# Attention with a gated SwiGLU on one core: the key and query products woven between the value products, and the first row of maxima written before the attention starts

## The chip, the core and the metric

The kernel runs on one core of a Trainium2 chip. The metric is the device time in microseconds of one execution; lower is better.

## What is computed

From x (1 x 2048 x 512), after a layer norm of each row:

```python
def _A_ref(x, wqkv, wo):                       # H = 32 heads, Dh = 16
    q, k, v = qkv[0], qkv[1], qkv[2]
    scores = jnp.einsum("bhqd,bhkd->bhqk", q, k) * Dh ** -0.5
    p = _softmax(scores, axis=-1)
    return einsum("bhqk,bhkd->bhqd", p, v).transpose(...).reshape(B, S, D) @ wo

def _B_ref(x, w1, w3, w2):                     # F = 1792
    return (_silu(x @ w1) * (x @ w3)) @ w2

xn = _layernorm(x)
return x + _A_ref(xn, wqkv, wo) * _silu(_B_ref(xn, w1, w3, w2))
```

All products are kept near f32 by splitting each operand into a high and a low part and multiplying three times (lo by hi, hi by lo, hi by hi).

## The kernel before, in words

**Two stages.** A prologue loads and normalises x in 16 tiles of 128 tokens, forms the value rows of all heads, and the key and query rows of the first 8 heads (two products of 512 tokens each per block). Then one long attention stage runs to the end, in which scores, row maxima, values and the whole gated feed-forward network share TensorE.

**The prologue (lines 449 to 693).** The 16 tiles make 4 blocks of 512 tokens. For each tile, `spread` takes mean and variance (VectorE, then a power on GpSimd), `norm` scales it (VectorE for the first tiles, ScalarE after), `transposed` turns it on TensorE and splits the result: the high part by a ScalarE copy, the low part by a VectorE subtraction. `token_values(b, i)` is one value product: 12 matmuls of 128x512; ScalarE copies the result out and its own DMA queue stores it. `token_rows(b, c)` is one key (c = 1) or query (c = 0) product of a block: 12 matmuls; ScalarE copies it out and GpSimd splits it (for the last block ScalarE and VectorE do). `keep_rows` stores these rows to DRAM, and `load_k`, `load_q` read them back, six DMAs each, into the layout that the scores need: everything that the first pair of heads multiplies goes through this round trip. `keep_tokens` stores a whole block of transposed tokens (two DMAs of 1 MB). These DMAs are on SyncE's queue.

**The order.** Block 0's four value products come first, inside the loop over the first four tiles. Then `for b in range(TB)` runs block by block: keys of the block, queries of the block, then (for blocks 1 to 3) its four value products. Between them `beside(b, n)` issues *maxima*: the shift of the softmax needs the row maximum of the scores, so `max_unit` (line 411) forms a 128x512 piece of the scores on half of TensorE and VectorE reduces it. 64 such units belong to the first half of the first pair of heads; the table `groups` spreads them in groups of 4, and two groups of 8 near the end. When all 64 are there, `max_rows` (line 424) reduces them, negates them on ScalarE, transposes them on TensorE, splits them and writes them by four DMAs as two more rows under the queries. Only then may the scores of the softmax itself be formed.

**The attention stage (from line 695).** The order in which TensorE gets its work is written out by hand in the table `ORDER_OF_ISSUE`, one letter per item: `f`/`F` a feed-forward matmul on the lower or upper half of the array, `m`/`M` a maximum unit, `s`/`S` a score product (line 706) with its exponential on ScalarE, `v` one chunk of value products (line 722, eight records), `R`/`r` the transposition of a row of maxima, `o` an output product. Small and capital letters stand for the two halves, which run side by side. TensorE takes its instructions in that order and waits where an operand is not there. A planner (`Model`) only decides buffers and small side tasks. The results of a letter stand in one of seven PSUM banks until VectorE or ScalarE has taken them out. Before, `rows` starts with the first row of maxima still to be transposed: the table's first `R` does it.

```python
for b in range(TB):              # lines 643 to 693, cut
    token_rows(b, 1)             # keys
    token_rows(b, 0)             # queries
    for i in range(TB):
        run(token_values(b, i))  # blocks 1 to 3
        beside(b, 2 + i)
```

Of the kernel before, what the change touches and what calls it, by code (L numbers as in the profile page):

```python
# [51 lines left out]
    "MfMfMfMfMffMfMfMffMffMfMfMffRfMfmFFfFmFFfFffFffFmFFFmFfffMfMfMmfFFFfFffFffFFFssfFmFFFffMfSffMsFFmfFS"  # L52
    "fFmSfFfSfMsFfmFsFfFFmsFFmMmvvsMfSfMfSfFFmSfFmFsFmFfSfMfFsFFfsMfSFfmFfFfMfSfMfSfSffMFsFfmFsFmFsFFfmFs"
    "FmFfSfFFmmMvvSmmMSmvvSmfSfMfSfMfSfmFsFFfmSFfsFmFsfFMsfFmFSfFmFfSmFfMmvvsMsSsSvvRmSfSfMFfsFfMfSFfsFmF"
    "SffMFsfFmSfFFmsFFfsMsFfsMvvsSSsmMvvFmsFmFsFFsFmfFfSfMSffMfSfFMfsFMffSffFSmFFffMSffmFFsFmFsfFsFMFfsFm"
    "sFFfMsFfMFffSfMfMmvvSssSmFmFvvSmMmMsvvMsFmFsfFsFfMSffFmSFfSfmSFffMfSFfmfFFfMfSfMfSfSffMsFfFmFsFFmsFF"
    "fmFsFmFsFFffMfMMfmSvvSmsMMmvvsMmFFsFfFsfMsFfFmSfFSfmFSfFfsMFfFfmFfMfMmMvvvRfSfMfSfMfSfMFfsFFmfSsFFfm"
    "FsFfFmSfFmFsFfFfMmMvvmSfFmSsFFffMFsfFmSFfsFmFFsfMFsfFmSFfMffMffSmMvvvFmsFmFFsFsFmsFmFFffSFmSFfMffSfM"
    "fSffMFfMMffMsvvmSfSfMfSfFFmfSFfMsFfsFMsfFFmsFFFmsFfMFffMfSmMvvsMmSFfFfFsfMFsFfmSfSfFmFsFfMsfFmFSfFmF"
    "fSfMfMmvvsMSfMfFsFffMsFfFmSFfFsmFFsFfmSFffSmFfSfFSsvvvvRfSMffSfMSffMfFsFmFfSFfFsmFsFFfmSFfFmsFFfMfmM"  # L60
    "vvmSSfmFfFFsfMFsFfmSFffSmFsFfFmSfFfMsFFffMSfMfmMvvSmMmsSvvMfSfMfSfMfSfMffSfSfMffMsFFfsFmFFsFmFsFfFmS"
    "fmFFssFFfMfSfFmSfFfMsfFsFMfSFfmSfFfMsFfMFfMffMmMvvvMmMssMvvmSmFsFsFmFFmFsFfFsfFFmSfFmFssFFfMfSfFmsFF"
    "fMsfFfMSfSFfmFfFfMfSfMfSSffMffMfSsMvvsSSmmMvvmFFsMmmSvvRsFFmFsFmFsFmFsFmFsFmFsFfSffFMsfFfMSFffSmFfSf"
    "MSffFmSfFMffFMfSfffMSfSffMMsvvsSsSsSvvvFmsFmFFsFsmFsFmFFsFmFsFFmFsfFFfmSFfFsmFfSfMfSfFmFMfffSfSfMMmv"
    "vMmMmSsvvmSFmFssFfFfMsFFfmSfFfSmFSfFfmSFffMfSfFfMFffMfSMffSfsFfMsFfFmFsFmFsFfFmFsFmFfFfMfMmMvvvmSSss"
    "MvvRsFFmFsFmsFFsmFfFSffMfSfFmSFffMsFFffMfMMfSmvvsMSfMfSffMffSfMsFfFmFsFmFfSsFFfmFFsfFmSFffFfMfSfMSff"
    "fMsFFmfFFsmFFsmFFfSfmFFsFmfFMmvvmSmMmSvvSmmMsSvMfSfMffSfMfSffSfMFsfFmSFfmFsFFsFmSffFMsfFFmFFffMfSfMf"
    "SfFsfFMsfFmFsFfFmFFsmFsFfFFmfMMfMmvvvvvmSfMfSfSfFFmfSfFMsfFFsMsFFfmfSFfMsfFmFSfFFffMSfffSfMSfmFfFFsm"
    "FsFFfmFsFFmFsfFFmSfSfrvvsMSfSmfFfFfMFsfFmSFfFsmFsFfMsfFmFSfFmFfMffMMmvvvsSSmSmvvMsfSMffSfFFmfSfFMsfF"
    "sFMsFFfmsFFMfsFFfmFMffMmMvvvSmMffFfSFffMFsmFfSFfFsmFFsFfSmfFmSfFFffMSffMfSffMfSfFsFmFsFfMsFFfmFsFmFs"  # L70
    "FfFFmMfMfMmvvvvsMfSmFfFFsfMsFFfmSFffSmFFsfMfSFfmSFffMFfFfMfSfffMSffMsFFsfFFmsFFmFsfFMfSfFsFmFfsFsSvv"
    "vvRMsFsmFFfFsfFmSFfsFmFsFfMSfFfmFFfMfSfffMSSffMfMffMmMvvvSmfMSffSfSfMfMffSfMfSfFFsmsFfFMsfFmFsFFmFsF"
    "sFFfmsFfFMsfFmFSfFFsmFsfFMSffMfSffFSffMfMmMvvvmSmMmSvvmFFsFmFsmFFssFmFFffSFmSFfmFsfFfMSfFSfmSffFMsFF"
# [73 lines left out]
def raw(ap):  # L147
    return ap.bitcast(F32)
# [1367 lines left out]
```

## Time and profile before

| what | value |
|---|---|
| time, median of 3 runs (lowest, highest) | 1715.81 us (1714.9, 1715.91) |
| time of the profiled execution | 1717.6 us |
| its span, first to last instruction | 1715.8 us |
| mean granted clock of TensorE | 0.997 |
| busy share: TensorE, VectorE, ScalarE, GpSimd | 99%, 80%, 72%, 51% |
| DMA | 181.07 MB, mean 106 GB/s |

The profiled execution's own time is 1.8 us above its span and 1.8 us above the median. A busy share of TensorE counts every matmul from its start to its modelled end, with matmuls overlapping, so 99% doesn't say that it works at its full rate: the spacing of matmul starts says that.

### The profile page before, as it was taken

The page shows a single profiled execution, that of the slowest core. Times are in us where ns is not written, and L with a number is a line of the kernel's source. Part 1 is how long each engine was busy: PE and PEld are TensorE (multiplying, and loading weights), DVE is VectorE, ACT ScalarE, POOL GpSimd, SP SyncE. Part 2 cuts the span into 40 slices and gives each one's busy share as a digit, 9 for nine tenths or more (in the row PEclk, how much of TensorE's full clock was granted, in tenths as well). Part 3 has the DMA queues.
Part 4 walks back from the last instruction along what each step waited for, and adds up shares of the span by engine and source line. Part 5 has one row for each costly group of instructions (what it writes and reads, how often), then busy time and mean ns, then how long its engine had stood idle before and what let it go on. Part 6 is the DMA issues. An engine that isn't in the chain of part 4 may idle for free.

```text
span 1715.8 us, 35891 instructions
## 1 busy us (share of the span) xinstructions
PE 1700.4 (99%) x13476; PEld 1125.9 (66%) x13476; DVE 1376.2 (80%) x2295; ACT 1228.0 (72%) x2446; POOL 868.4 (51%) x911
## 2 busy tenths in 40 slices
PE   8999999999999999999999999999999999999998
PEld 6766666666766666666666666666667666665456
DVE  5788888898887888887897888778788787889626
ACT  4338777777767777778777777777777777868870
POOL 7155463466456653565546762565366616653011
PEclk9999999999999999999999999999999999999999
DMA  7563433443344443422244452321433312421264
GB/s 261 200 206 93 125 96 86 106 114 59 87 153 104 118 96 100 106 64 59 83 119 123 129 124 82 97 70 51 105 91 77 81 38 61 116 78 30 81 208 145
DMA packets 170893, 181.07 MB, mean 106 GB/s; under 512 B 43872, under 2 KB 115552, under 8 KB 167744
## 3 DMA queue, kind: packets, MB, share of 16 engines
q1 hardware_dynamic: 167552, 172.76, 37.0%
q10 hardware_dynamic: 3168, 6.03, 1.0%
q8 instruction: 106, 1.74, 0.5%
q14 instruction: 67, 0.55, 0.1%
HBM read 131.56 MB, written 46.11 MB: 104 GB/s over the span
## 4 chain that ended last, share of the span: by engine, by line
PE 92%; issue 2%; DVE 2%; DMA 2%; SPq 1%; POOL 1%; ACT 0%; ACTq 0%; DVEq 0%; POOLq 0%
PE f L1023 32%; PE pv L722 26%; PE m L419 16%; PE e L706 15%; PE m L546 2%; DVE mp L421 1%; DMA wr<-in_A_wqkv_dram 1%; SPq L758 0%; DMA ovh<-o 0%; PE m L434 0%; DMA inh<-in_A_x_dram 0%; PE e L201 0%; PE m L519 0%; PE o L201 0%; PE e L205 0%
## 5 line engine op out<-in xcount | busy, mean ns | idle before, releaser
L421 DVE TENSOR_REDUCE mp<-m 128x1 f32<-128x512 f32 x2048 | 1277.6, 683 | 216.0 <-PE m L419 139.9
L709 ACT ACTIVATE pt<-e 128x512 f32<-128x512 f32 x2048 | 1058.4, 612 | 281.7 <-PE e L706 162.4
L419 PE MATMUL m<-ks,qs 62*128 62x512 f32 x2048 | 741.9, 413 | 4.7 <-DMA qs<-qk 3.2
L706 PE MATMUL e<-qs,ks 64*128 64x512 f32 x2048 | 737.6, 407 | 0.0
L722 PE MATMUL pv<-pt,vt 128*17 128x512 f32 x4096 | 479.5, 594 | 0.0
L419 PEld LDWEIGHTS m<-ks,qs 62*128 62x128 f32 x2048 | 349.3, 184 | 123.6 <-issue 39.3
L706 PEld LDWEIGHTS e<-qs,ks 64*128 64x128 f32 x2048 | 349.4, 185 | 101.9 <-issue 34.9
L722 PEld LDWEIGHTS pv<-pt,vt 128*17 128x17 f32 x4096 | 100.2, 97 | 251.0 <-issue 245.0
L1023 PE MATMUL f<-xtl,wh 64*128 64x512 f32 x504 | 183.9, 392 | 0.0
L1023 PE MATMUL f<-xth,wl 64*128 64x512 f32 x504 | 178.9, 394 | 0.0
L1023 PE MATMUL f<-xth,wh 64*128 64x512 f32 x504 | 175.7, 392 | 0.0
L1023 PE MATMUL f<-wh,hs 64*128 64x512 f32 x528 | 165.8, 392 | 0.0
L866 POOL TENSOR_TENSOR h<-g,h 128x512 f32<-128x512 f32 x56 | 72.1, 1287 | 182.5 <-ACT h L862 182.4
L1023 PE MATMUL f<-xth,xel 64*128 64x512 f32 x440 | 160.5, 394 | 0.0
L1023 PE MATMUL f<-xth,xeh 64*128 64x512 f32 x440 | 160.5, 393 | 0.0
L1023 PE MATMUL f<-xtl,xeh 64*128 64x512 f32 x440 | 160.4, 391 | 0.0
L340 POOL TENSOR_TENSOR wl<-wr,wh 128x512 fp32r<-128x512 f32 x105 | 135.2, 1288 | 8.8
L1023 PE MATMUL f<-xeh,hs 64*128 64x512 f32 x368 | 121.3, 395 | 0.4 <-POOL hs L868 0.4
L340 POOL TENSOR_TENSOR xel<-wr,xeh 128x512 fp32r<-128x512 f32 x87 | 112.1, 1289 | 7.3
L339 POOL TENSOR_SCALAR xeh<-wr 128x512 fp32r<-128x512 f32 x87 | 53.8, 619 | 100.6 <-PE m L419 42.6
L1023 PE MATMUL f<-wl,hs 64*128 64x512 f32 x264 | 97.3, 392 | 0.0
L1023 PEld LDWEIGHTS f<-wh,hs 64*128 64x128 f32 x528 | 92.3, 185 | 4.8 <-POOL hs L868 1.0
(241 smaller groups left out, 2134.6 us busy)
## 6 DMA issues: line engine op xcount, KB each, us to landing
wr<-in_B_w_dram SPq DMA_DIRECT2D x168, 256.0 KB
qs<-qk SPq DMA_DIRECT2D x186, 64.0 KB
ks<-qk SPq DMA_DIRECT2D x90, 128.0 KB
ovh<-xt SPq DMA_DIRECT2D x36, 256.0 KB
ovl<-xt SPq DMA_DIRECT2D x36, 256.0 KB
wr<-in_A_wqkv_dram SPq DMA_DIRECT2D x30, 256.0 KB
qk<-ch SPq DMA_DIRECT2D x24, 256.0 KB
qk<-c SPq DMA_DIRECT2D x24, 256.0 KB
```

Source lines behind the costliest of these rows:

```text
L339: nc.gpsimd.tensor_scalar(hi, t, 1.0, 1.0, op0=ALU.mult, op1=ALU.mult)
L340: nc.gpsimd.tensor_sub(lo, t, raw(hi))
L419: nc.tensor.matmul(ps, qs[p % 2][64 * h:64 * h + KM, q0:q0 + P], ks[p % 2][64 * h:64 * h + KM, c * 512:(c + 1) * 512], start=True, stop=True)
L421: nc.vector.reduce_max(mp[p, half][:, h, qt, c:c + 1], ps, axis=AX.X)
L546: nc.tensor.matmul(ps, lhs, wv[k][h == 1], start=n == 0, stop=n == len(three) - 1)
L706: nc.tensor.matmul(ps, ks[p % 2][64 * h:64 * h + KR, k * P:(k + 1) * P], qs[p % 2][64 * h:64 * h + KR, q0:q0 + 512], start=True, stop=True)
L709: done = nc.scalar.activation(pt, ps, AF.Exp, scale=DH ** -0.5)
L722: nc.tensor.matmul(pv[32 * j:32 * j + VW, :], vt[2 * p // GH][:, key, 2 * p % GH + j % 2, :], pt, start=key < 2 if last else k == 0, stop= ...
L866: nc.gpsimd.tensor_mul(h2, g, h2)
L1023: nc.tensor.matmul(ps, left[r], right[r], start=starts and lane == 0, stop=ends and lane == 1)
```

## The change

The prologue's loop is replaced by a `plan`: a list of twenty products (key, query, value), each with the tiles to be turned after it, the number of maxima to be issued after it, and the small tasks then due. The key and query products of all blocks now stand between value products: k0 q0 v v k1 q1 v k2 q2 v v k3 q3 v v v and four more v. The value products still go in the order of the blocks. The 64 maxima come in twelve groups of 3 to 6. The first row of maxima is finished in the plan: its maximum and negation after the 17th product, its transposition and its DMAs after the 18th; the attention stage starts with `ready = {0: 0.5}` and no row to do. The last block's tokens and rows are split on GpSimd; `norm` of tiles 1 to 3 goes to ScalarE; one weight's split goes from GpSimd to VectorE; `keep_tokens` issues on ScalarE's queue instead of SyncE's; `vrow` has four buffers instead of two; block 1's tokens have buffers of their own. The table `ORDER_OF_ISSUE` is wholly new: the same number of `f`, `m`, `s` and `o`, 512 `v` and `r` as before, and 31 `R` and `r` for 32. Its letters form 200 runs of `v` and `r` where there were 206. Of the table the first line of either version is shown; the removed loop is cut, since the kernel before shows it.

```diff
@@ -49,98 +49,98 @@
 
 
 ORDER_OF_ISSUE = (
-    "MfMfMfMfMffMfMfMffMffMfMfMffRfMfmFFfFmFFfFffFffFmFFFmFfffMfMfMmfFFFfFffFffFFFssfFmFFFffMfSffMsFFmfFS"
...
+    "MffSfMfSfMSffMSffSMffSffMfsMffMfMfMsFFfsFFffFsFFmsFFsFfmSFffMFffMfSfSffMFsfFmFsFmFsFmFFfsFFmfSmFFfMf"
...
 )
 
 
@@ -497,7 +497,7 @@
             rs = pro.tile([P, 1], F32, tag="rs", name="rs", bufs=6)
             nc.gpsimd.tensor_tensor(rs, ve, minus, op=ALU.pow)
             nb = None
-            if t >= TB:
+            if t > 0:
                 nb = pro.tile([P, 1], F32, tag="nb", name="nb", bufs=6)
                 nc.gpsimd.tensor_scalar(nb, mv[:, 0:1], rs, -1.0, op0=ALU.mult, op1=ALU.mult)
             of[t] = mv, rs, nb
@@ -513,14 +513,20 @@
         def transposed(t, xn):
             b, tt = divmod(t, 4)
             if tt == 0:
-                xts[b] = xt_pair(keep) if b % 2 else rows2 if b else even_pair()
+                xts[b] = rows2 if b == 2 else (even_pair, lambda: xt_pair(pro), None, lambda: xt_pair(keep))[b]()
             ps = bank("m")
             for k in range(KC):
                 nc.tensor.transpose(ps[:, k * P:(k + 1) * P], xn[:, k * P:(k + 1) * P], ident)
             hi, lo = (v[:, :, tt * P:(tt + 1) * P] for v in xts[b])
             src = ps.rearrange("p (k t) -> p k t", k=KC)
-            nc.scalar.copy(hi, src)
-            nc.vector.tensor_sub(lo, src, raw(hi))
+            if b < TB - 1:
+                nc.scalar.copy(hi, src)
+                nc.vector.tensor_sub(lo, src, raw(hi))
+            else:
+                xc = pro.tile([P, KC, P], F32, tag="xc", name="xc", bufs=2)
+                nc.scalar.copy(xc, src)
+                nc.gpsimd.tensor_scalar(hi, xc, 1.0, 1.0, op0=ALU.mult, op1=ALU.mult)
+                nc.gpsimd.tensor_sub(lo, xc, raw(hi))
 
         def split_w(i, sub=None):
             w = wraw.pop(i)
@@ -548,8 +554,8 @@
                     yield
             t = b * 4 + i
             v = ps.rearrange("p (h d) -> p h d", h=H)
-            nc.scalar.copy(vrow[t % 2][:, :, 0:DH], v)
-            nc.scalar.dma_start(v_d[t], vrow[t % 2].rearrange("p h d -> p (h d)"))
+            nc.scalar.copy(vrow[t % 4][:, :, 0:DH], v)
+            nc.scalar.dma_start(v_d[t], vrow[t % 4].rearrange("p h d -> p (h d)"))
             nc.scalar.copy(vt[0][:, t, :, 0:DH], v[:, 0:GH, :])
 
         nc.gpsimd.memset(raw(ks[0]), 1.0)
@@ -561,10 +567,10 @@
         spread(1)
         transposed(0, xn.pop(0))
         busy(6)
+        split_w(2)
+        split_w(3, nc.gpsimd)
         norm(1)
-        split_w(2, nc.gpsimd)
-        split_w(3, nc.gpsimd)
-        vrow = [pros.tile([P, H, VW], F32, name=f"vrow{i}") for i in range(2)]
+        vrow = [pros.tile([P, H, VW], F32, name=f"vrow{i}") for i in range(4)]
         for v in vrow:
             nc.gpsimd.memset(v[:, :, DH:VW], 1.0)
         nc.gpsimd.memset(room_v(0)[:, :, :, DH:VW], 1.0)
@@ -576,13 +582,12 @@
             if t < 3:
                 transposed(t + 1, xn.pop(t + 1))
             norm(t + 2)
-            if t < 2:
-                split_w(KC + t, nc.gpsimd)
+            if 0 < t < 3:
+                split_w(KC + t - 1, nc.gpsimd)
             for n in range(2):
                 load_x(8 + 2 * t + n)
-            if t > 1:
-                nc.gpsimd.memset(*next(blank))
             run(products)
+        nc.vector.memset(*next(blank))
         nc.vector.memset(pv, 0.0)
         for n in range(2):
             nc.vector.tensor_add(picks[:, 2 * n:2 * n + 2], each[:, 0:2], each[:, 2:4])
@@ -590,18 +595,7 @@
         early = [(c, qt, h) for c in range(4) for qt in range(8) for h in range(2)]
         early.sort(key=lambda e: (max(e[0], e[1] // 4), e[0] < e[1] // 4, e))
         early = iter([(0, 0, 4 * qt + c, h) for c, qt, h in early])
-        groups = {(1, 1): 4, (1, 2): 4, (1, 4): 4, (1, 5): 4, (3, 3): 8, (3, 4): 8}
-        groups.update({(2, n): 4 for n in range(6)})
...
         first_rows = max_rows(0, 0)
-
-        def beside(b, n):
-
-            for _ in range(groups.get((b, n), 0)):
-                max_unit(*next(early))
-            if (b, n) == (TB - 1, 4):
-                next(first_rows)
-                next(first_rows)
 
         def token_rows(b, c):
 
@@ -611,14 +605,10 @@
                 run(split3(ps, [w[:, k, :] for w in wqk[c]], (hi[:, k, :], lo[:, k, :]), k == 0, k == KC - 1))
             sh = pros.tile([P, 512], F32R, tag="sh", name="sh", bufs=3)
             sl = pros.tile([P, 512], F32R, tag="sl", name="sl", bufs=3)
-            if b == TB - 1:
-                nc.scalar.copy(sh, ps)
-                nc.vector.tensor_sub(sl, ps, raw(sh))
-            else:
-                sc = pros.tile([P, 512], F32, tag="sc", name="sc", bufs=2)
-                nc.scalar.copy(sc, ps)
-                nc.gpsimd.tensor_scalar(sh, sc, 1.0, 1.0, op0=ALU.mult, op1=ALU.mult)
-                nc.gpsimd.tensor_sub(sl, sc, raw(sh))
+            sc = pros.tile([P, 512], F32, tag="sc", name="sc", bufs=2)
+            nc.scalar.copy(sc, ps)
+            nc.gpsimd.tensor_scalar(sh, sc, 1.0, 1.0, op0=ALU.mult, op1=ALU.mult)
+            nc.gpsimd.tensor_sub(sl, sc, raw(sh))
             made_rows[b, c] = sh, sl
 
         made_rows = {}
@@ -629,68 +619,67 @@
 
         def keep_tokens(b):
             for s in range(2):
-                nc.sync.dma_start(raw(xt_d[b][s]), raw(xts[b][s]).rearrange("p k t -> p (k t)"))
+                nc.scalar.dma_start(raw(xt_d[b][s]), raw(xts[b][s]).rearrange("p k t -> p (k t)"))
 
         def more_tokens(n):
 
-            if n < NT:
-                transposed(n, xn.pop(n))
-                if n + 2 < NT:
-                    norm(n + 2)
-                if n + 4 < NT:
-                    spread(n + 4)
-
-        for b in range(TB):
-            cols = slice(b * 512, (b + 1) * 512)
-            last = b == TB - 1
-            token_rows(b, 1)
...
+            transposed(n, xn.pop(n))
+            if n + 2 < NT:
+                norm(n + 2)
+            if n + 4 < NT:
+                spread(n + 4)
+
+        def cols(b):
+            return slice(b * 512, (b + 1) * 512)
+
+        def keys_here(b):
+            return lambda: keep_rows(b, 1), lambda: load_k(0, cols(b))
+
+        def queries_here(b):
+            return lambda: keep_rows(b, 0), lambda: load_q(0, 0, cols(b)) if b < TB // 2 else None
+
+        def blank_next():
+            nc.gpsimd.memset(*next(blank))
+
+        def weights_first():
+            wts.pump(KC)
+            wts.fill()
+
+        plan = [
+            ("k", 0, (4, 5), 0, keys_here(0)[:1]),
+            ("q", 0, (6,), 0, ()),
+            ("v", 0, (7,), 0, queries_here(0)[:1] + keys_here(0)[1:] + queries_here(0)[1:]),
+            ("v", 1, (8,), 0, (lambda: keep_tokens(0),)),
+            ("k", 1, (9, 10), 0, ()),
+            ("q", 1, (11,), 4, keys_here(1)),
+            ("v", 2, (12, 13), 5, queries_here(1) + (lambda: keep_tokens(1),)),
+            ("k", 2, (14,), 5, ()),
+            ("q", 2, (15,), 5, keys_here(2)),
+            ("v", 3, (), 6, queries_here(2)),
+            ("v", 0, (), 6, (blank_next,)),
+            ("k", 3, (), 6, (lambda: load_q(1, 0), lambda: keep_tokens(2))),
+            ("q", 3, (), 6, keys_here(3)),
+            ("v", 1, (), 6, queries_here(3) + (lambda: load_q(0, 1),)),
+            ("v", 2, (), 6, (blank_next, blank_next, wts.start)),
+            ("v", 3, (), 6, (weights_first,)),
+            ("v", 0, (), 3, (lambda: next(first_rows), lambda: next(first_rows))),
+            ("v", 1, (), 0, (lambda: next(first_rows), lambda: next(first_rows, None))),
+            ("v", 2, (), 0, ()),
+            ("v", 3, (), 0, ()),
+        ]
+        done = 0
+        for what, n, tiles_, maxima_, then in plan:
+            if what == "v":
+                run(token_values(1 + done // TB, n))
+                done += 1
             else:
-                keep_rows(b, 1)
-            if b == 0:
-                keep_tokens(b)
...
+                token_rows(n, int(what == "k"))
+            for _ in range(maxima_):
+                max_unit(*next(early))
+            for t in tiles_:
+                more_tokens(t)
+            for e in then:
+                e()
 
     ring = ctx.enter_context(tc.tile_pool(name="ring", bufs=1))
     work = ctx.enter_context(tc.tile_pool(name="work", bufs=1))
@@ -1264,12 +1253,12 @@
 
 
 
-    ready = {}
+    ready = {0: 0.5}
     opened, closed = [], []
     count = {"S": 0, "M": 64, "V": 0, "chunks": 0, "phase": 1}
     keys = {0: 0.0}
     rooms = []
-    rows, outs = [[3.0, first_rows, 2, 0]], []
+    rows, outs = [], []
     stored = {}
     pv_free = 0.0
     multiplied = {}
```

## Rows read from the trace of the kernel before

**Rows 1.** Who waited for whom, PE, 130 to 1650 us: us, times, longest

```profile
PE f L1023 <- POOL hs L868: 0.4, 1, 0.4
```

**Rows 2.** The chain that ended last, in order: start us, us, what

```profile
124.74 1.84 PE pv L722 x16
...
199.44 2.70 PE pv L722 x24
```

**Rows 3.** Timeline of PE, 15 to 48 us: start us, us, engine line op, [idle before]

```profile
15.94 0.50 PE L546 MATMUL m<-wvl,xeh 128*128 128x512 f32 x1 [0.84 <-ACT xeh L522]
...
31.17 0.50 PE L201 MATMUL e<-xth,wkl 128*128 128x512 f32 x1 [1.48 <-ACT xth L522]
32.39 0.50 PE L203 MATMUL e<-xtl,wkh 128*128 128x512 f32 x1 [0.72 <-DVE xtl L523]
...
40.15 0.47 PE L419 MATMUL m<-ks,qs 62*128 62x512 f32 x1 [1.76 <-DMA qs<-qk]
42.05 1.19 PE L419 MATMUL m<-ks,qs 62*128 62x512 f32 x3 [1.43 <-DMA qs<-qk]
...
44.51 0.63 PE L546 MATMUL m<-wvl,xth 128*128 128x512 f32 x1
...
47.07 0.63 PE L546 MATMUL m<-wvl,xth 128*128 128x512 f32 x1
```

**Rows 4.** Stretches: us, PE, PEld, DVE, ACT, POOL busy, PEclk, DMA share, GB/s

```profile
29.00:31.00 2.00, 0.69 (x7) 0.46 (x5) 1.67 (x5) 2.00 (x5) 1.14 (x4) 1.00 1.04 416
...
41.00:48.00 7.00, 5.95 (x17) 4.48 (x18) 3.86 (x8) 1.30 (x2) 1.24 (x4) 0.51 0.58 194
```

**Rows 5.** Timeline of PE, 79 to 104 us: the first matmul of six products

```profile
79.83 0.50 PE L546 MATMUL m<-wvh,ovl 128*128 128x512 f32 x1
...
83.44 0.50 PE L201 MATMUL e<-xth,wkl 128*128 128x512 f32 x1
...
90.67 0.50 PE L546 MATMUL m<-wvh,xtl 128*128 128x512 f32 x1
...
93.53 0.39 PE L546 MATMUL m<-wvh,xtl 128*128 128x512 f32 x1
...
98.22 0.50 PE L546 MATMUL m<-wvh,xtl 128*128 128x512 f32 x1
...
103.07 0.50 PE L546 MATMUL m<-wvh,xtl 128*128 128x512 f32 x1
```

**Rows 6.** Timeline of PE, 106 to 119 us: the entry into the attention stage

```profile
106.00 0.50 PE L1023 MATMUL f<-xth,xel 64*128 64x512 f32 x1
...
111.75 0.28 PE L434 MATMUL m<-ident,nm 128*16 128x128 f32 x1
...
117.19 0.39 PE L1023 MATMUL f<-xtl,xeh 64*128 64x512 f32 x1
...
118.11 0.39 PE L1023 MATMUL f<-xth,xeh 64*128 64x512 f32 x1
...
118.39 0.39 PE L706 MATMUL e<-qs,ks 64*128 64x512 f32 x1
```

**Rows 7.** Timeline of DVE, 97 to 127 us

```profile
97.49 9.11 DVE L421 TENSOR_REDUCE mp<-m 128x1 f32<-128x512 f32 x15
...
113.94 0.27 DVE L438 TENSOR_TENSOR ml<-m,mh 16x128 fp32r<-16x128 f32 x1
```

**Rows 8.** Timeline of SyncE's issues (SPq), 33 to 87 us

```profile
33.14 4.05 SPq L398 DMA_DIRECT2D ks<-qk  x6
...
78.97 3.47 SPq L325 DMA_DIRECT2D wr<-in_A_wqkv_dram  x2
86.61 0.37 SPq L325 DMA_DIRECT2D wr<-in_B_w_dram  x1
```

**Rows 9.** The page, costliest groups: a split on POOL, count, busy us, mean ns

```profile
L340 POOL TENSOR_TENSOR wl<-wr,wh 128x512 fp32r<-128x512 f32 x105 | 135.2, 1288 | 8.8
...
L339 POOL TENSOR_SCALAR xeh<-wr 128x512 fp32r<-128x512 f32 x87 | 53.8, 619 | 100.6 <-PE m L419 42.6
```

More of the change, by code (lines that the diff above doesn't have):

```diff
@@ L57 @@
[L57 to L61, printed above, removed]
@@ new lines @@
+    "vRsMfMFsfFfSfFmFSfFmSffFFmFfFmFmmFmFvvvMfSfMffSfMfSffSfMsFFfmSfFFmsFsFFmfFSfMFsFfmFFfMffSMffSfSffMsF"
+    "fFmFsFFmsFfFmFsFFmsFFfMfMfMfmMvvvsMsMfFFfFsfMsFFfmSfFsFmFfSfMsfFFmSFfmFfMffMmMvvvSmfSfMSffFFmfSFfMsF"
+    "fsFMsFFfmsFfFMsFfmFFffMMmSvvmSsFmFsFFffMsFfFmSfFSfmFSffMfSFfmSFfsfFMFfmmMvvRSmsFFfmFsFFfmSFfFsmFFsfM"
+    "sFfFmSffMFfMfMfSmvvmSmSMmvvMsMffSSffMfSffMsFfFMfsFFmfSfSFfmFFsFmFsfFMsFFffMfSffMSffMsFFmFsFsFfMfFsFm"
+    "sFFfMsFFfmFMffMmMvvSmsSFmFmvvvSmsFmFfFfSfMsFfFmSfFfSmSFffMSfFfmFFffMfSfMfSffSfMsFFfmFsFFmsFFfmFsFFms"
@@ new lines @@
+    "FfFfMfMfSmMvvvSmSmsMvvvRSmfSFffMfSfFMsFfSfMsFFfmSffFMsFMfFfsFFmsFFffMsfFFmsFFfMsFfmFFsmFFfSfMFfsMfFf"
+    "FMfMfmMvvSmfSmFFfFsfMsFFfmSfFfSmFfSFfmSFfFmsFFffMSfSfsMvvmSsMMmvvmSMmSsvMfSffMSfMffSfMfSSffMfMfsFFfF"
+    "smFsFFmFsfFFmSfmFFssFfFMsFfFmSfFfMsFFfsMfSFfmSFfMffFfMfMmMvvvSssSsMvvSmsMMmvvfMfSMffSMffSfsFFmFFsfMs"
+    "fFmFFsFmFsFfSfMfSFfmFsFmFsFfSfFmSfFfMsFfFmFfSfMfSfMfFmrvmSSssMvvsMmMmSvvmSmFFsfFFsfMsFfMfSfMfFsFmFfS"
+    "sFfFmFfSfMsFfmFFsFmfFSfmFFsmFFfSffMFffSfMfSfMMmvvMsmMSsvmFsFFmFsmFFsmFFsFmFsFfSFffMsfFmFSfsFFmFsFfMf"
@@ L144 @@
+    "MfMMmvvvMsMfFsFfFsfMFsFfmSfFfSmFsFFfmSfFFmsFSfFfmFfSfMFsfFmFsFfMsFfFFsmSvsMmMsSvSmMffSMsvsMmSSmvSmmS"
+    "SfMfvMsMsMsvsMMffSsMvRMsFmSsvmSsSMmvmSmSMsvmSsSMmvmSMsmFSvSmmSSmvFmFsFmFssFFmFmFsSmvMsSmmSvmSsFsMosS"
+    "mFsMvSmSssMvsSSsMoSsmSvvSsSsmMvSmMmFsFsFFsMFsFMsFFMSsMvMsMSMSsSvsSsMMsvMSMSsvMsMSSsvsMSSSSSSvvvvRooS"
+    "sSssFosSsSSsvSsSsosSSsSsovSsSsSsovvSssSsSoSsSssSooovvvvsSsSSsSvovsSSssSovSsSsSsoSsSssSooooooovvvvv"
 )
@@ L592 @@
         early = iter([(0, 0, 4 * qt + c, h) for c, qt, h in early])
-        groups = {(1, 1): 4, (1, 2): 4, (1, 4): 4, (1, 5): 4, (3, 3): 8, (3, 4): 8}
-        groups.update({(2, n): 4 for n in range(6)})
-        groups.update({(3, n): 4 for n in range(2)})
         first_rows = max_rows(0, 0)
-        def beside(b, n):
-            for _ in range(groups.get((b, n), 0)):
-                max_unit(*next(early))
-            if (b, n) == (TB - 1, 4):
-                next(first_rows)
-                next(first_rows)
         def token_rows(b, c):
```

206 lines of the change are left out of this document (77 added, 129 removed).

## The prediction, written before the changed kernel was run

> **What bounds the kernel now.** I read the page first: TensorE counts as busy for 99% of the span, every other engine for 80% or less. Then who waited for whom on TensorE alone: in the 1520 us from 130 us on it idles visibly for less than a microsecond [rows 1]. So the attention stage runs at TensorE's pace, and what a letter of the table costs there is the spacing of matmul starts: 0.23 us on each half of the array, 0.115 us per half matmul (four steps from 117.19 to 118.11 us) [rows 6], and 0.86 us per chunk of values plus 0.12 us for each run of them (1.84 us for two, 2.70 us for three) [rows 2]. The change alters none of the counts of letters that matter. What it can win lies in the first 120 us, and the timeline of TensorE shows there what is lost.
>
> It is lost in four places. (a) Between 29 and 42 us TensorE stands four times: 1.48 + 0.72 us for block 1's turned tiles, then 1.76 + 1.43 us for the first queries on their way through DRAM [rows 3]. That is 5.4 us. The order causes it: keys and queries of two blocks are formed with nothing else to do, and the first maxima follow at once. (b) After that idling the granted clock falls: 0.51 over 41 to 48 us, the lower of the two levels (1.2 GHz, not 2.4) [rows 4]. Value matmuls start there every 0.43 us (six from 44.51 to 47.07) [rows 3] instead of 0.24 us (twelve from 90.67 to 93.53) [rows 5]. (c) The two groups of eight maxima: a value product with a group of four takes 3.61 us (79.83 to 83.44), one alone 2.86 us, one with a group of eight 4.85 us (98.22 to 103.07) [rows 5]. So four maxima cost 0.75 us, eight 1.99 us. (d) The entry into the attention stage: from 106.00 to 118.39 us, the first score, TensorE goes through 77 letters [rows 6], 76 half matmuls and one transposition of a row.
>
> **The change, part by part.**
>
> *Waits (a).* In the plan two value products and three tiles stand between q0 and k1, and k1 and q1 before the first maximum. Block 1's last tile then has a value product and a tile ahead of k1, 3 us, where it was late by 1.5 us. From q0 to the first maximum the kernel before has k1, q1 and a few tiles, and waits 5.4 us in all until 42.05 us; now two value products stand there besides, 2 x 2.86 us [rows 5]. They cover the waits with 0.3 us to spare. Gain 5.4 us; ends 2.2 us, if only the turned tiles come in time, and 5.4 us. A remainder of the wait is charged below.
>
> *Clock (b).* Nine value matmuls at 0.19 us too much are 1.7 us; the 2 us or so between 42.05 us and the first of them, at the lower level too, give another 0.9 us. Gain 2.6 us if no idling replaces the old one; ends 0 and 3.0 us, half of the 5.95 us busy there [rows 4].
>
> *Maxima (c).* Before: 12 groups at 0.75 and 2 at 1.99 us, 13.0 us. After: 0.115 us per unit more or less than four, so 0.64 us for the group of three, 0.75 for the one of four, 3 x 0.87 and 7 x 0.98 for those of five and six: 10.9 us. Gain 2.1 us. VectorE must keep up: it needs 0.607 us per maximum (15 in 9.11 us) [rows 7], 3.64 us for six, and TensorE gives it 2.86 + 0.98 = 3.84 us. It just does. If not, groups of five and six lie between the prices of four and eight (1.06 and 1.37 us), 14.2 us in all: a loss of 1.2 us.
>
> *Entry (d).* 76 half matmuls at 0.115 us are 8.7 us, the row's turn about 0.3 us (a step longer than its 0.28 us), against 12.4 us less half a step: some 3.2 us lost. VectorE is the reason: it works off maxima without a pause, and the low part of the row, one small instruction, comes at 113.94 us, 2.2 us after the transposition [rows 6, 7]. The new table begins `MffSfMfSfM`: one maximum in five letters instead of one in two, with scores taken out by ScalarE beside them. Gain 3.0 us. New there: the third letter but one is a score, so TensorE now needs the row at once. Before, 6.6 us lay between the row's transposition and the first score [rows 6], and about 1.6 us of that was VectorE's backlog; 5.0 us remain. The plan puts two value products, 5.7 us, in between. I charge 0.5 us; ends 0 and 2 us.
>
> *Runs.* Six runs of values fewer: 6 x 0.12 us at least, twice that if entering costs as leaving does. Gain 1.0 us. What else the new table does to 1580 us can't be read from the old trace: both ways 3 us, taken at nothing, since the counts are the same.
>
> *Start.* Norms of tiles 1 to 3 leave VectorE, one split leaves GpSimd. One stall of 0.84 us is to be had [rows 3]; I take 0.4 us.
>
> *What is added.* GpSimd splits the last block's four tiles: 4 x (0.62 + 1.29) = 7.6 us [rows 9], and two rows more, 3.8 us. It is half idle, and between tile 15 and k3, which needs it, stand two products with six maxima each, 7.7 us. Nothing, unless those go away; then up to 7.6 us. The two DMAs of 1 MB per block go past ScalarE's queue instead of SyncE's. For block 0 this is a delay: they were issued ahead of the first rows and now come after them, while the queries are being read back. Before, the engines were full from 29 us on, 416 GB/s [rows 4]; 2 MB take 5.0 us at that rate. SyncE needed 4.05 us for the six key loads, with a wait in it for the stored rows [rows 8], so this path gets freer at its start and fuller at its end. And the ninth maximum needs block 1's keys one value product after the first eight could be had. I charge 1.0 us for late rows; ends 0 and 6 us.
>
> **Sum.** 5.4 + 2.6 + 2.1 + 3.0 + 1.0 + 0.4 = 14.5 us won, 1.5 us charged, 13.0 us net. From the profiled execution's 1717.6 us that gives 1704.6 us; the median of the runs stands 1.8 us under that execution, so **1702.8 us**.
>
> **The rivals.**
>
> *Late rows.* The big stores run beside the loads, the first maxima wait some 3.5 us for queries or keys, the clock falls again (2.6 us lost), and the row is 1 us late at the entry: 6 to 7 us of the 13 go, 1709 us. For it: TensorE takes its work in order, and the transfer engines were full when the old order stored block 0 [rows 4]. Against it: the stores now start when x has been read, and the loads no longer wait behind them. The Trainium skill ("DMA: Bandwidth & Descriptors", section "Issuing engines are not separate DMA queues") speaks for this rival: DMAs of whatever issuing engine end on the same 16 engines and interleave, and a second issuer saves only issue time. By that rule alone the move to ScalarE buys the loads no transfer time and the time would be this rival's; no row here shows both queues busy side by side, so it stays untested.
>
> *Nothing gained.* The new order of the attention stage costs 0.025 us more per chunk, 512 x 0.025 = 12.8 us, as the old trace can't exclude: 1715 us. Against it: the stage's price per letter is fixed by TensorE, and the counts are equal.
>
> *Slower, through ScalarE's queue.* After the last pair of 1 MB stores SyncE needed from 78.97 to 86.98 us for three issues [rows 8], 0.37 us each when free: it stood for 6.9 us. If ScalarE stands like that after each of three pairs, nothing it should copy out moves: 20.7 us, and free banks carry TensorE over part of it. From 13.0 us uncovered on the gain is gone; with all of it uncovered, 1723 us. Against it: SyncE's issues came at once behind the stores, while ScalarE's next one is a value row, a product or 3 us later.
>
> **How the numbers follow.** The forecast, 1698 to 1706 us by its own ends, has 0.60. Late rows 0.22, nothing gained 0.07, slower 0.07; 0.04 for still faster than 1697, if the table's own 3 us come on top. The range 1697 to 1712 us leaves out the last three, about 0.18. A measurement of this kernel can tell about 0.2% from no change, 3.4 us: faster means under 1712.4 us. That is 0.60 + 0.04 and nearly all of the late rows, 0.84; same 0.08; slower 0.08.
>
> **What would show it.** Right: the first feed-forward matmul at 92 to 95 us instead of 106.00, no stretch of granted clock at the lower level after the start, no idling of TensorE over 1 us between 22 us and there, reductions on VectorE with gaps at the entry, and a score within 1 us of the entry. Wrong: TensorE waiting for `qs` or `ks` before the first groups of maxima, or for the row at the first score; `vrow` copies on ScalarE that start late behind its issues; or the entry earlier by 12 us and the end not.

## The result: 0.25% slower, and the profile after

The changed kernel takes 1720.13 us (median of 10 executions, 1718.11 to 1722.54), the kernel before on the same chip 1715.86 us (1714.02 to 1718.52): a ratio of 1.0025, with a 95% interval of 1.0015 to 1.0035. The forecast was 1702.8 us. The profiled execution took 1721.93 us, its span is 1719.8 us, and its mean granted clock is 0.996.

Who waited for whom comes first. The list of TensorE in the changed kernel is (us in total, times, longest); of the two waits on `qs` one, 2.14 us, lies in the prologue, the other at 924 us:

```profile
PE m L419 <- DMA qs<-qk: 4.6, 2, 2.5
PE m L419 <- DMA ks<-qk: 3.4, 1, 3.4
PE m L419 <- ACT g L835: 2.2, 1, 2.2
...
PE m L552 <- ACT vt L559: 1.2, 3, 0.4
```

The waits of [rows 3] from 31 to 42 us are gone, and others have come. TensorE's timeline says where (start us, us, engine, line, operation):

```profile
45.00 0.71 PE L419 MATMUL m<-ks,qs 62*128 62x512 f32 x3 [2.14 <-DMA qs<-qk]
...
61.10 0.47 PE L552 MATMUL m<-wvh,xtl 128*128 128x512 f32 x1
...
65.43 0.50 PE L552 MATMUL m<-wvh,ovl 128*128 128x512 f32 x1 [0.40 <-ACT vt L559]
...
84.77 0.76 PE L419 MATMUL m<-ks,qs 62*128 62x512 f32 x1 [3.43 <-DMA ks<-qk]
85.47 0.80 PE L552 MATMUL m<-wvh,ovl 128*128 128x512 f32 x1
...
90.33 0.62 PE L552 MATMUL m<-wvh,ovh 128*128 128x512 f32 x1
...
108.71 0.50 PE L1012 MATMUL f<-xth,xel 64*128 64x512 f32 x1
...
109.21 0.47 PE L695 MATMUL e<-qs,ks 64*128 64x512 f32 x1
...
530.28 0.50 PE L419 MATMUL m<-ks,qs 62*128 62x512 f32 x1 [2.19 <-ACT g L835]
```

The reader is to see four things. The first queries are late by 2.14 us and block 3's keys (the last ones) by 3.43 us, inside the prologue. After each of these waits the matmuls come more slowly: the twelve of the value product at 85.47 us lie 0.44 us apart on average (to 90.33), where at the upper level they lie 0.24 us apart [rows 5]. A value product with its group of six lasts 4.33 us (61.10 to 65.43), 0.40 us of it a wait for ScalarE's copy of v, where the forecast had 3.84. And the first feed-forward matmul comes at 108.71 us, not at 92 to 95 us: 2.7 us later than before [rows 6]. The first score follows it after 0.5 us, as forecast. The table by stretch has the clock in its seventh number, ahead of the DMA share and the GB/s: 0.57 is the lower level for most of the stretch.

```profile
41.00:48.00 7.00, 4.86 (x21) 3.22 (x20) 5.99 (x14) 3.37 (x6) 4.78 (x7) 0.89 0.69 264
...
83.00:91.00 8.00, 6.23 (x15) 4.21 (x17) 1.69 (x3) 0.23 (x2) 0.00 (x0) 0.57 0.56 170
```

What the late loads stood behind is seen on the two queues, SyncE's (SPq) first:

```profile
36.75 4.88 SPq L407 DMA_DIRECT2D qs<-qk  x6
...
50.53 6.84 SPq L407 DMA_DIRECT2D qs<-qk  x6
...
75.55 0.34 SPq L618 DMA_DIRECT2D qk<-sl  x1
81.72 2.37 SPq L398 DMA_DIRECT2D ks<-qk  x5
...
527.18 0.58 SPq L815 DMA_DIRECT2D qk<-ch  x1
```

And ScalarE's issues and copies:

```profile
36.94 0.33 ACTq L622 DMA_DIRECT2D xt<-xeh  x1
39.26 0.33 ACTq L622 DMA_DIRECT2D xt<-xel  x1
...
72.89 0.33 ACTq L622 DMA_DIRECT2D xt<-ovh  x1
73.31 0.39 ACTq L622 DMA_DIRECT2D xt<-ovl  x1
...
529.64 0.59 ACT L835 COPY g<-f 128x512 f32<-128x512 f32 x1 [3.89 <-DMA qk<-ch]
```

Two of the three pairs of 1 MB stores (L622) meet rows that are waited for. Beside the first, six query loads take 4.88 us to issue. Before the change they took 2.73 us, the next six 6.51 us:

```profile
37.24 2.73 SPq L407 DMA_DIRECT2D qs<-qk  x6
...
45.29 6.51 SPq L407 DMA_DIRECT2D qs<-qk  x6
```

So the 6.84 us of the loads beside the second pair (52.65 and 53.29 us) are hardly more than before, and TensorE waits for none of them. The third pair is issued at 72.89 and 73.31 us, just ahead of the row stores of k3. The last of these is issued at 75.55 us, and the loads that need it only at 81.72 us. The last line of the first and of the second of these three fences belongs to a stall in the attention stage, taken up below.

### The profile page after: what moved, and what is told of

Read it like the earlier page. It is cut to its first block, busy times and chain, and to the rows that moved or that the text cites. A ratio compares the mean times of both kernels' runs of the same rounds, so it can differ in the third digit from the quotient of the medians.

```text
span 1719.8 us, 35915 instructions
## 1 busy us (share of the span) xinstructions
PE 1699.1 (99%) x13476; PEld 1128.0 (66%) x13476; DVE 1371.2 (80%) x2288; ACT 1232.1 (72%) x2449; POOL 877.9 (51%) x926
## 4 chain that ended last, share of the span: by engine, by line
PE 90%; DMA 3%; issue 2%; POOL 2%; SPq 1%; DVE 1%; ACT 1%; ACTq 0%; POOLq 0%; DVEq 0%
PE f L1012 31%; PE pv L711 26%; PE m L419 15%; PE e L695 15%; PE m L552 2%; DMA xin<-in_A_x_dram 1%; DMA inh<-in_A_x_dram 1%; DMA qs<-qk 1%; DMA qk<-sl 0%; POOL sl L611 0%; PE m L434 0%; DMA last<-in_A_wo_dram 0%; DMA ks<-qk 0%; SPq L747 0%; PE o L201 0%
## 5 line engine op out<-in xcount | busy, mean ns | idle before, releaser
L1012 PE MATMUL f<-xth,wh 64*128 64x512 f32 x504 | 181.3, 392 | 0.0
```

Source lines behind the costliest of these rows:

```text
L1012: nc.tensor.matmul(ps, left[r], right[r], start=starts and lane == 0, stop=ends and lane == 1)
```

## The experiments

The theory: the pairs of token stores, 2 MB put out at once, take from the prologue what its new order wins, and the new table loses more at its stalls than it wins at the entry. The rivals are that the queue is at fault and not the place, that the 6 MB cost the same however they are put out, and that the order itself is worth nothing. The kernel before ran beside each: its medians lie between 1714.6 and 1716.0 us. The runs were taken on three chips (e1 to e4, e13 and e14; e5 to e8; e10 to e12), so a difference of 1 us between two of these sets says little; the ratios are safer. The first f is read from the one profiled execution of a run. With the same prologue it differs by 1.6 us between the changed kernel and e3 and by 2.6 us between e1 and e4, so it is a coarse measure too.

| run | median us | ratio to before, 95% interval | first f, us |
|---|---|---|---|
| e1 stores later | 1714.08 | 0.9983 to 1.0001 | 104.44 |
| e2 stores on SyncE | 1721.24 | 1.0022 to 1.0047 | 109.22 |
| e3 old table | 1718.08 | 1.0004 to 1.0021 | 107.12 |
| e4 both e1 and e3 | 1714.59 | 0.9985 to 1.0003 | 101.83 |
| e5 stores cut | 1711.15 | 0.9959 to 0.9981 | 97.95 |
| e6 cut, groups of 5 and 7 | 1710.24 | 0.9957 to 0.9981 | 97.61 |
| e8 as e6, old table | 1709.07 | 0.9952 to 0.9977 | 97.69 |
| e10 as e6, chunk rows on ScalarE | 1750.28 | 1.0179 to 1.0215 | 97.22 |
| e11 as e6, spliced table | 1707.83 | 0.9941 to 0.9966 | 96.94 |
| e12 before, stores cut | 1714.88 | 0.9987 to 1.0005 | 102.25 |
| e13 as e11, cut but not spread | 1718.67 | 1.0005 to 1.0024 | 108.71 |
| e14 as e11, pieces on SyncE | 1713.49 | 0.9979 to 0.9997 | 99.84 |

**e1, the stores later.** The pairs go to three later steps of the plan:

```diff
-            ("v", 1, (8,), 0, (lambda: keep_tokens(0),)),
+            ("v", 1, (8,), 0, ()),
...
-            ("v", 3, (), 6, queries_here(2)),
+            ("v", 3, (), 6, queries_here(2) + (lambda: keep_tokens(0),)),
```

> The changed kernel with the three pairs of 1 MB token stores moved in the plan, still on ScalarE's queue: block 0's from the 4th product to the 10th, block 1's from the 7th to the 14th, block 2's from the 12th to the 15th, where no row that TensorE waits for is on its way. Theory 1 (the stores fill the transfer engines while rows are stored and read back): the waits for queries (4.6 us) and keys (3.4 us) shrink to under 1 us each, both stretches at the lower clock before 100 us go, the first feed-forward matmul comes at 96 to 100 us instead of 108.7, and the time is 1708 to 1712 us. Rival (the rows are late by their own path: GpSimd's splits, SyncE's order, the round trip): the waits stay at 6 us or more in sum, the first feed-forward matmul at 106 us or later, 1718 us or more.

The early waits went, and 6 us with them, but the first f came only at 104.44 us (in the slowest of the run's 11 executions). Two pairs now follow each other on ScalarE's queue, and the engine stands there:

```profile
85.83 0.33 ACTq L622 DMA_DIRECT2D xt<-ovl  x1
86.20 0.58 ACT L557 COPY vrow<-m 128x512 f32<-128x512 f32 x1 [4.01 <-PE m L419]
89.08 0.33 ACTq L558 DMA_DIRECT2D v<-vrow  x1
```

The copy of v ended at 86.8 us, its store was issued at 89.08 us, and the next copy, which frees the bank, came behind it: TensorE's next value product waited 3.58 us, and from 89 to 96 us the granted clock was 0.54. This is the mechanism of the slower rival, at one place.

**e2, the stores on SyncE's queue.** The queue of before, the places of after:

```diff
-                nc.scalar.dma_start(raw(xt_d[b][s]), raw(xts[b][s]).rearrange("p k t -> p (k t)"))
+                nc.sync.dma_start(raw(xt_d[b][s]), raw(xts[b][s]).rearrange("p k t -> p (k t)"))
```

> The changed kernel with the token stores at its own places in the plan, but issued on SyncE's queue again. If the place is what costs (theory 1), the waits for queries and keys stay, within 2 us in sum of the changed kernel's 8.0, and the time is 1718 to 1723 us. If ScalarE's queue is what costs (its issues hold up its copies), the waits and the low clock go and the time falls to 1712 us or less.

It is 1.1 us above the changed kernel, within the two runs' spread. The waits are still there, now on keys. Two of these three lie in the prologue, 3.58 and 3.66 us, where the changed kernel has 2.14 and 3.43; the third, 0.72 us, at 924 us:

```profile
PE m L419 <- DMA ks<-qk: 8.0, 3, 3.7
```

So for stores of 1 MB the queue makes no difference to the time that can be measured; the place does (e1). The rule cited with the rival of late rows (the Trainium skill, "DMA: Bandwidth & Descriptors", section "Issuing engines are not separate DMA queues") agrees: a second issuer gave the loads no transfer time.

**e3, the table of before under the new prologue.** The 92 lines of `ORDER_OF_ISSUE` are those of before, nothing else.

> The changed kernel's prologue with the table of the kernel before. If the new table brought the two stalls seen at 528 and 922 us (2.2 and 2.5 us, with a fall of the clock after the first), they go, some 6 us; the old entry with a maximum in every second letter costs about 2.5 us again: 1716 to 1718 us. If the new table costs nothing, the old one makes it 2 us slower: 1722 us or more.

It is 2.05 us faster than the changed kernel. The prologue's waits stay (2.18 us on queries at 44.59, 3.42 us on keys at 84.38) and the attention stage has no stall.

**e4, e1 and e3 together.** Both edits.

> The stores moved as in the first run of this set and the table of the kernel before. If both causes are real and independent the gains add: 8 to 12 us from the prologue and 3 to 4 us from the table, 1705 to 1709 us. If the old table only works at its old distance from the prologue, it stalls as well and the time stays at 1709 us or above.

1714.59 us, no better than e1: the gains don't add, and the attention stage has no wait of over 1 us either, so neither forecast's reason holds. The 3.40 us wait behind ScalarE's queue stands at 89.64 us here too; in this trace the granted clock falls later, in the entry (0.57 from 108 to 112 us). Why the 2 us of e3 don't show in the median stays open. Moving the pairs exchanges one wait for another.

**e5, the stores cut and spread.** Twenty-four pieces of 256 KB, one or two a step, on ScalarE's queue:

```diff
+        parts = iter([(b, s, k) for b in range(TB - 1) for s in range(2) for k in range(KC)])
+        def keep_parts(n):
+            for b, s, k in [next(parts) for _ in range(n)]:
+                nc.scalar.dma_start(raw(xt_d[b][s])[:, k * 512:(k + 1) * 512], raw(xts[b][s])[:, k, :])
...
+        stores = [0, 0, 0, 1, 1, 1, 1, 2, 1, 1, 2, 2, 1, 2, 1, 1, 2, 1, 2, 2]
...
+            keep_parts(stores.pop(0))
```

> The changed kernel, its six token stores of 1 MB cut into 24 pieces of 256 KB, issued on ScalarE's queue one or two a group from the first value product of block 2's tokens on, in place of three pairs. If the time is lost because a pair of stores (2 MB at once) holds what the prologue waits for, the rows when it lies early and ScalarE at issue when it lies late, pieces hold neither: no wait of a maxima matmul on qs or ks over 1 us before the first f, no copy of ScalarE late by over 1 us, no stretch of product matmuls at 0.4 us apart after 40 us, first f at 97 to 102 us, and the kernel at 1706 to 1711 us (the first stall of the new table, at 528 us, stays). If the rival holds that the six MB in themselves cost some 6 us between 40 and 100 us, wherever and however they are issued, because the loads and stores of the prologue already take the DMA engines' time there, the first f comes no earlier than 103 us and the time stays at 1713 to 1716 us.

First f 10.8 us earlier than in the changed kernel, the median 9.0 us lower. The same 6 MB go out: the rival that they cost their time wherever they lie has fallen. Left are the group of six after a value product and the stall of the table, here at 521 us:

```profile
76.69 0.46 PE L419 MATMUL m<-ks,qs 62*128 62x512 f32 x1 [0.44 <-DMA ks<-qk]
...
81.46 0.50 PE L552 MATMUL m<-wvh,ovl 128*128 128x512 f32 x1 [0.43 <-ACT vt L559]
...
85.79 0.50 PE L552 MATMUL m<-wvh,xtl 128*128 128x512 f32 x1 [0.41 <-ACT vt L559]
...
97.95 0.50 PE L1016 MATMUL f<-xth,xel 64*128 64x512 f32 x1
...
521.21 0.50 PE L419 MATMUL m<-ks,qs 62*128 62x512 f32 x1 [2.89 <-ACT g L839]
```

**e6, five maxima after a value product, seven after k3 and q3.** The group behind the 17th product, a value product too, grows from three to six. In the plan, cut:

```diff
-            ("v", 3, (), 6, queries_here(2)),
+            ("v", 3, (), 5, queries_here(2)),
...
-            ("k", 3, (), 6, (lambda: load_q(1, 0),)),
+            ("k", 3, (), 7, (lambda: load_q(1, 0),)),
```

> As the run with the stores cut into pieces, and five maxima after a value product where the changed kernel has six, seven after block 3's key and query products. In the changed kernel a value product with six takes 4.33 us and the next product's first matmul waits 0.4 us for ScalarE's copy of v, since six maxima and the product fill all seven banks; five leave one bank. If that wait is what makes a group of six dear, value product and five come at 3.8 to 3.9 us a group, the waits on vt go, and the kernel gains 1 to 2 us on the run with the cut alone. The rival: the six maxima cost 0.16 us each of TensorE's own time wherever they stand (key and query products too), and then the two runs are within 0.5 us.

```profile
56.52 0.47 PE L552 MATMUL m<-wvh,xtl 128*128 128x512 f32 x1
...
60.38 0.50 PE L552 MATMUL m<-wvh,ovl 128*128 128x512 f32 x1
...
64.24 0.50 PE L201 MATMUL e<-xth,wkl 128*128 128x512 f32 x1
...
68.46 0.50 PE L201 MATMUL e<-xth,wql 128*128 128x512 f32 x1
...
88.52 0.50 PE L552 MATMUL m<-wvh,xtl 128*128 128x512 f32 x1 [0.38 <-ACT vt L559]
```

A product with five takes 3.86 us and no longer waits for v's copy; the key product with seven takes 4.22 us (64.24 to 68.46), and seven reductions at VectorE's 0.607 us [rows 7] are 4.25 us. The wait on v's copy is left behind the one value product that now has six (88.52 us). From 56.52 to the 18th product at 88.52 us it is 32.0 us, where e5 takes 33.4: 1.4 us won. But the first f comes only 0.34 us earlier, less than it varies between runs with this prologue (97.61, 97.69 and 96.94 us in e6, e8 and e11), and the times don't tell the runs apart. Expected were 1 to 2 us.

**e8, e6 with the table of before.**

> As the run with pieces and groups of five and seven, with the order table of the kernel before. If the new table is a gain at the entry (2.6 us by the trace, its 13 us from first f to first value product against 18.7 us) that it gives back at two stalls of the attention stage (528 and 922 us, some 6 us with the clock that falls behind the first), then this run has no wait of over 1 us on g or qs after 200 us, and is within 3 us of the run with the new table: faster by 1 to 3 us if the stalls weigh more. If the rival holds, that the stalls come only when the prologue ends where it did in the changed kernel, the new table has lost its stalls in the run with pieces, and the old table is slower by 2 to 4 us.

No wait over 1 us is left after 17 us, and the median is 1.2 us below e6's, with intervals that overlap, though the first score comes 12.2 us behind the first f (109.88) instead of 1.3 us.

**e10, the rows of the attention stage on ScalarE's queue.** The stall at 521 to 530 us begins with `ch`, a chunk of projected rows. In the changed kernel its store is issued at 527.18 us, behind eight stores of attention rows and four loads that began at 520.42 us. The copy `g` needs the same buffer and waits 3.89 us for the store, TensorE 2.19 us for the copy.

```diff
-                    nc.sync.dma_start(raw(qk_d[rbk][s])[:, b * 512:(b + 1) * 512], v)
+                    nc.scalar.dma_start(raw(qk_d[rbk][s])[:, b * 512:(b + 1) * 512], v)
```

> The run with pieces and groups of five and seven under the new table, with the stores of the projected rows of the attention stage (24 pairs, ch and c) moved from SyncE's queue to ScalarE's. In that run such a pair was issued at 518.40 us, some 5 us after GpSimd had split it, because eight stores of attention rows and four loads of sums stood ahead of it on SyncE's queue; the copy g, which takes the same buffer, waited 5.0 us for it, and TensorE 3.3 us for the copy. If the queue is the cause, the wait on g is gone, the granted clock stays at the upper level from 500 to 540 us, and the kernel gains 3 to 4.5 us: 1705.5 to 1707.5 us. The stall at 917 us (a load of queries, 2 us) is not touched. If the rival holds, that the new table puts too much on GpSimd or on the DMA engines there (their share is 1.0 from 500 to 510 us), the store is late on ScalarE's queue too, ScalarE stands behind it, and the time stays at 1709 to 1712 us.

Neither time was right: 40 us slower than e6. The wait on g is gone, as it would be if SyncE's queue was its cause, but ScalarE pays, so much that this run alone proves little. Its own list and TensorE's:

```profile
ACT pt L702 <- POOL c L814: 24.6, 10, 2.5
```

```profile
PE e L699 <- ACT pt L702: 18.9, 10, 2.3
PE m L419 <- ACT pt L702: 7.5, 2, 5.4
```

The store waits for GpSimd's split, and every exponential behind it waits too: 40 us over 24 pairs are 1.7 us a pair.

**e11, both tables.** The first 619 letters of the new table, then the old one from where it has issued as much:

```diff
-    "sFfFmSffMFfMfMfSmvvmSmSMmvvMsMffSSffMfSffMsFfFMfsFFmfSfSFfmFFsFmFsfFMsFFffMfSffMSffMsFFmFsFsFfMfFsFm"
...
+    "sFfFmSffMFfMfMfSmvvffRvSfFmSsFFffFsfFmSFfsFmFFsfMFsfFmSFfMffMffSmMvvvFmsFmFFsFsFmsFmFFffSFmSFfMffSfM"
...
```

> The run with pieces and groups of five and seven, with the new table's first 619 letters and the old table's from there on (two letters f and one R put in at the seam). If the new table wins only at the entry (2.6 us) and loses only at its two stalls, this run has both: first score within 1.5 us of the first f, no wait of over 1 us on g or qs, and 1705.5 to 1707.5 us. If the rival holds, that a time won at the entry is lost again whatever the table, because what is worked off early there is missing as cover later, the run comes no nearer than 1708 to 1710 us, as with the old table alone (1709.1).

1707.83 us: 0.47% faster than the kernel before and the lowest median of all. It is 2.4 us under e6's and 1.2 us under e8's; the intervals of the ratios overlap with both. The query loads beside the first pieces took 2.85 us again, and no stretch from 0 to 120 us has a granted clock below 1.00:

```profile
35.80 2.85 SPq L407 DMA_DIRECT2D qs<-qk  x6
...
95.49 0.63 SPq L446 DMA_DIRECT2D qs<-ml  x1
```

**e12, the kernel before with the cut alone.** The same `keep_parts`, one or two pieces after each product of blocks 1 to 3 of the old loop.

> The kernel before, with nothing of the change but the cut: its six token stores of 1 MB in 24 pieces of 256 KB, on ScalarE's queue, one or two after each product of blocks 1 to 3. If the order of the change is worth what was worked out for it (value products between the key and query products, maxima spread), the waits of the old order at 29 to 42 us stay for the greater part, with the low clock behind them, and this run gains at most 2 us: 1713 to 1715.5 us, against 1709.1 with the order of the change and the same table. If the rival holds, that the pairs of stores were what cost the kernel before its 5.4 us there, and the order in itself is worth nothing, this run comes to 1708 to 1711 us.

No gain in the median. The turned tiles of [rows 3] are late by the same amounts, but the first queries by 0.57 us only, where it was 1.76 + 1.43:

```profile
31.12 0.50 PE L201 MATMUL e<-xth,wkl 128*128 128x512 f32 x1 [1.48 <-ACT xth L522]
32.34 0.79 PE L203 MATMUL e<-xtl,wkh 128*128 128x512 f32 x1 [0.71 <-DVE xtl L523]
...
40.91 0.70 PE L419 MATMUL m<-ks,qs 62*128 62x512 f32 x3 [0.57 <-DMA qs<-qk]
```

So of the 5.4 us that the old order stood, 2.6 us go with the stores alone, in this trace. The plan (its order, with the groups, the row and the splits that came along) wins the 5.8 us between e12 and e8, which both have the old table and cut stores; the cut lets it. Its parts aren't told apart.

**e13, the pieces not spread.** The 24 pieces of e11, eight at once at the changed kernel's three places:

```diff
-        stores = [0, 0, 0, 1, 1, 1, 1, 2, 1, 1, 2, 2, 1, 2, 1, 1, 2, 1, 2, 2]
+        stores = [8 * (n in (3, 6, 11)) for n in range(20)]
```

> The run with pieces, groups of five and seven and the spliced table (1707.8 us), with the 24 pieces of 256 KB no longer spread: eight at once at the three places where the changed kernel issues its pairs of 1 MB. If what cost the time is how much is put out at once, ahead of the rows that are waited for, the cut alone does not help: the waits on qs and ks and the lower clock of the changed kernel come back and the first f comes at 104 to 109 us, 1714 to 1720 us in all; ScalarE issues for 2.6 us and more at each place. If the size of one transfer is what costs (a 1 MB store that, once begun, holds an engine from the small rows), 256 KB pieces let the rows between them wherever they are issued, and the time stays at 1707 to 1710 us.

10.8 us over e11, first f at 108.71 us, as in the changed kernel: the cut alone doesn't help, and the amount put out at once costs. But the waits have changed hands, which was not expected. The loads are hardly late (0.65 us), while ScalarE stands at its issues and its copies wait. So this run doesn't show that 1 MB stores and 256 KB pieces delay the loads alike:

```profile
36.95 2.18 ACTq L624 DMA_DIRECT2D xt<-xeh  x3
39.78 2.89 ACTq L624 DMA_DIRECT2D xt<-xel  x4
...
76.78 4.31 ACTq L624 DMA_DIRECT2D xt<-ovl  x4
```

```profile
59.75 0.50 PE L201 MATMUL e<-ovh,wql 128*128 128x512 f32 x1 [1.92 <-ACT sc L609]
...
81.83 0.50 PE L419 MATMUL m<-ks,qs 62*128 62x512 f32 x1 [1.79 <-ACT sc L609]
```

**e14, the pieces on SyncE's queue.** `nc.sync` for `nc.scalar` in `keep_parts`.

> The run with spread pieces, groups of five and seven and the spliced table (1707.8 us), with the pieces on SyncE's queue, at the same places, in place of ScalarE's. If place and amount decide and the queue doesn't (as the whole stores on SyncE's queue suggested, 1721.2 against 1720.1 us), the time stays within 2 us of 1707.8, with rows issued 0.4 us later behind each piece. If the rival holds, that pieces beside the loads do no harm only because a queue of their own interleaves with the rows', the rows wait behind the pieces on SyncE's queue, the waits on qs and ks return with the lower clock, and the time is 1712 us or more.

5.7 us over e11: here the rival was right. The first f comes 2.9 us later than in e11, behind two waits, and the granted clock is 0.83 from 100 to 110 us:

```profile
80.44 0.47 PE L419 MATMUL m<-ks,qs 62*128 62x512 f32 x1 [1.32 <-ACT vt L559]
81.94 0.73 PE L419 MATMUL m<-ks,qs 62*128 62x512 f32 x4 [1.03 <-DMA ks<-qk]
```

SyncE issues the low part of the maxima row at 102.15 us, behind pieces and weights, where e11 does at 95.49 us, and the first score waits:

```profile
102.15 0.63 SPq L446 DMA_DIRECT2D qs<-ml  x1
```

```profile
104.00 0.46 PE L699 MATMUL e<-qs,ks 64*128 64x512 f32 x1 [3.43 <-DMA qs<-ml]
```

A second queue didn't help the stores of 1 MB (e2), but for the pieces it kept the rows' issues from standing behind them.

## Why the prediction was wrong

The forecast was 13.0 us faster; measured are 4.3 us slower. Four steps were mis-sized by 17.8 us in sum, where 17.3 us are to be explained; the first two are measured by runs, the third read from traces, the fourth argued.

**What is added, the token stores: 8 us.** The step "I charge 1.0 us for late rows; ends 0 and 6 us" failed, and it decides the sign. The cut and spread give back 9.0 us under either table (1720.13 to 1711.15, and e3 to e8, 1718.08 to 1709.07, this with the groups of e6). Only block 0's pair had been worked out. The pair of block 2 stands ahead of k3's rows, and costs 3.43 us and a whole value product at the lower clock. The rival of late rows named the cause and priced it at 6 to 7 us, by one stretch of low clock where there are two. Its chance, 0.22, was too small: the transfers issued beside a wait were in the diff, and the place of each against the row stores could have been written down step by step.

**Runs and entry, the new table: 5.5 us.** Won were to be 2.5 us net at the entry and 1.0 us by fewer runs; the changed kernel is 2.05 us faster with the old table (e3). The entry itself worked: TensorE has its first score 0.5 us after the first f, and the spliced table's median is 1.2 us under the old table's, within the intervals. From the first f to the end of the span the changed kernel takes 1611.1 us, the kernel before 1609.8, e3 1609.0 and e11 1608.6. "What else the new table does to 1580 us ... taken at nothing, since the counts are the same" failed. Equal counts say nothing on when the queues carry stores: two stalls, 2.19 us at 530 us with the clock behind it, and 2.5 us at 924 us for queries, are new. The clock is 0.66 from 530 to 535 us. The store that the first stands behind is issued behind twelve others on SyncE's queue, and with it off that queue the wait is gone (e10). Of the second only the load is known to be late. Both are gone under the old and the spliced table (e3, e8, e11).

**Maxima (c): 2.5 us.** VectorE kept up, as worked out, but "if not, groups of five and six lie between the prices of four and eight" was the case that came, by another cause: v's copy frees the bank too late. In e5 four of the five value products with six came at 4.33 to 4.38 us, not 3.84, and the fifth, which waited 0.44 us for keys besides, at 4.74. After key and query products six cost what was forecast (72.34 less 64.67 us for two: 3.83 us each).

**Clock (b), counted twice: 1.8 us.** The sum was made on an execution 1.8 us above the median, then the 1.8 us was taken off again. Among the 75 executions of the kernel before that were timed beside the experiments, the 24 with a mean granted clock of 0.999 have a median of 1714.4 us, the 23 with 0.997, as the profiled one, 1717.15 us. So a good part of the 2.6 us was likely this execution's own. That would also account for e12, whose first f comes 3.75 us earlier than in that profile and whose median doesn't come earlier; it is argued from the clocks, not tried. Whether the waits of [rows 3] are as long in the faster executions of the kernel before, no trace shows.

**Right**, as far as one trace can say, was the size of what the prologue can win: with the stores out of the way the first f comes at 97.95 us (e5), 8.05 us earlier than before, where 5.4 + 2.6 + 2.1 + 0.4 is 10.5 us, less the 2.5 us of the groups. It was not all the order's, as (a) had it: 2.6 us of the waits go without it (e12). The start isn't seen: the stall of 0.84 us that it was to shorten is 0.88 us in the changed kernel and 1.12 us in e5. And the sign "92 to 95 us" for the first f doesn't follow from the sum: 106.00 less 10.5 us, and 1.0 us charged, is 96.5 us, since the entry's gain lies behind the first f. GpSimd's added splits cost nothing that can be seen. The rival by ScalarE's queue came true in part, in e1 and e13, and hidden in the changed kernel: behind the third pair a copy of v ended at 81.08 us and its store was issued at 83.55 us, while TensorE waited longer still for the keys; nothing speaks for the table costing something in every chunk.

What stays open: the stall at 917 to 924 us, and stores between 256 KB and 1 MB, above all the six of 1 MB put out singly at six places, which would tell the spread from the cut. A third buffer for `g` and `ch`, the direct cure of the stall behind SyncE, wasn't tried.

## What to carry to other kernels

When products are pulled together to hide a round trip through DRAM, write the large stores that aren't urgent into the same plan, piece by piece: 2 MB at once undid 9 us of an order that was right, and neither a later place, another queue nor the cut alone cured it; small pieces, spread, on a queue without urgent rows did. Don't store from ScalarE what another engine still has to make: it stands until then, and all its exponentials with it. When a table of issue order is replaced whole, look for what its queues carry at the places where the counts say nothing, and try the old table from some letter on.

## What the runs showed that was not expected

An engine that issues DMAs stood while much was out: ScalarE needed 4.31 us for four issues of 256 KB in e13, right behind four others (some 0.33 us each when free). Moving 48 small stores to ScalarE cost 40 us. The wait of 3.43 us in the changed kernel brought the lower granted clock with it, eleven spacings of 0.44 us in place of 0.24: 2.2 us more.
